# Two products of a linear-attention layer, put on 32-wide tiles of the TensorE array

## The chip, the cores and the metric

The kernel runs on one core of a Trainium2 chip. The metric is the device time of one execution in microseconds; medians of several runs are quoted. TensorE is the engine for matrix products; its results go to PSUM, a small memory that VectorE or ScalarE, the engines for element-wise work, must empty. A difference under 2% counts as "same".

## The reference

Four layers are applied in turn to an input of 2048 rows by 1024 columns: linear attention (A), a gated product (B), A again, B again. Only A matters here:

```python
phi = lambda t: jnp.where(t > 0, t + 1, jnp.exp(t)) + 1e-6
pq, pk = phi(q), phi(k)                          # 32 heads of 32 columns
kv  = jnp.einsum("bhsd,bhse->bhde", pk, v)       # one 32 x 32 block per head
z   = jnp.einsum("bhsd->bhd", pk)
num = jnp.einsum("bhqd,bhde->bhqe", pq, kv)
den = jnp.einsum("bhqd,bhd->bhq", pq, z)[..., None] + 1e-6
return (num / den, heads side by side) @ wo      # (shortened)
```

The kernel never forms `num`. Per layer it forms G = x^T·pk (the "g units"), from it k^T v = wv^T·G per head (the "kv units"), then M = (k^T v)·wo, a 1024 x 1024 matrix, and the output is (pq/den)·M. Each head needs only a 32 x 32 block of k^T v.

## The kernel before

The parts that the change touches. The array is 128 x 128, a chunk `c` holds four heads, and the products of one head with another are computed too and then masked away.

```python
def both(ps, lhsT, rhs, start, stop):            # two matmuls of 512 columns
    for n in range(2):
        nc.tensor.matmul(out=ps[:, n, :], lhsT=lhsT, rhs=rhs[:, n * NB:(n + 1) * NB], start=start, stop=stop)

def kv_unit(m):                                  # m = 0..7, accumulates over m
    def run():
        # ... psum tile "kv" [128, 8, 128] at m == 0
        for c in range(KD):
            nc.tensor.matmul(out=acc[0][:, c, :], lhsT=wkv[:, m, c * P:(c + 1) * P],
                             rhs=Gs[m % 2][:, c * P:(c + 1) * P], ...)
        if m == KD - 1:
            for h in range(2):                   # keep the four 32x32 diagonal blocks of each chunk
                nc.vector.tensor_tensor(out=KVb[:, 4 * h:4 * h + 4, :], in0=acc[0][:, 4 * h:4 * h + 4, :],
                                        in1=mask[:].unsqueeze(1).to_broadcast([P, 4, P]), op=ALU.mult)

def q_with_m(t, later):                          # last q unit, M woven in
    # ... PSUM tiles
    for c in range(KD):
        if c == 2: step(c)                       # step: two matmuls of the q unit
        pm = pss[(0, 1, 0, 2, 1, 0, 2, 0)[c]]
        both(pm, KVb[:, c, :], wo[c], True, True)     # M: 16 matmuls of 128x512 in all
        # ... copy pm to M on ScalarE or VectorE
        if c != 2: step(c)
    # ...

# ... order of the units on TensorE:
do([g[0], g[1], z_sum, kv[0]] + d(0) + [g[2], kv[1]] + d(1, 2) + [g[3], kv[2]] + ...)
# ...
do(d(8) + [q[2], g[6], kv[5]] + ... + [g[7], kv[6], q[5], kv[7], q[6]])
q_with_m(15, later)
```

`d(t)` is the division by `den`: about 4.2 us of VectorE work per block of 128 rows. `Gs` has two buffers.

## Time and profile before

| | before |
|---|---|
| device time, median | 1630.16 us (4 runs, 1629.41 to 1630.41) |
| profiled span | 1627.6 us |
| TensorE busy | 1622.9 us, 7649 matmuls |
| a 512-column matmul, start to start | 0.216 us |
| a kv unit, first start to the next unit's first start | 0.447 us |
| "stretch": first z matmul to first output-projection matmul, one layer | 76.52 us |

From the page of the kernel before, its busy times, then the chain of waits by engine:

```profile
span 1627.6 us, 17734 instructions
PE 1622.9 (100%) x7649; PEld 741.2 (46%) x7649; DVE 609.3 (37%) x889; ACT 289.3 (18%) x387; POOL 55.2 (3%) x141
...
PE 99%; DMA 0%; DVE 0%; issue 0%; SPq 0%
```

A busy TensorE may still be waiting inside, because a matmul's recorded duration (379 ns for 512 columns) overlaps the next one's. Start times decide. The timeline of TensorE alone has start, duration of the merged piece, engine, source line, operation, operands, shapes and count:

```profile
133.77 7.07 PE L202 MATMUL ps<-R,R 128*128 128x512 bf16 x32
140.68 0.61 PE L303 MATMUL kv<-GL,W 128*128 128x128 bf16 x8
141.12 3.62 PE L202 MATMUL ps<-W,xT 128*128 128x512 bf16 x16
```

The 32 matmuls of a g unit take 140.68 - 133.77 = 6.91 us, 0.216 us each. The eight of the kv unit take 0.45 us and the next unit starts at once. There is no bubble. The same view where M is made:

```profile
173.54 0.59 PE L202 MATMUL pm<-W,KVb 128*128 128x512 bf16 x2
173.98 0.59 PE L202 MATMUL ps<-W,xT 128*128 128x512 bf16 x2
174.41 0.59 PE L202 MATMUL ps<-W,KVb 128*128 128x512 bf16 x2
...
180.02 0.59 PE L202 MATMUL ps<-W,xT 128*128 128x512 bf16 x2
180.45 1.24 PE L202 MATMUL ps<-R,xT 128*128 128x512 bf16 x5
```

M (operand `KVb`) and the last q unit alternate, every pair 0.43 us after the one before. From 173.54 to 180.45 are 6.91 us for 32 matmuls, half of them M's: 16 x 0.216 = 3.46 us.

### The profile page before, as it was taken

The numbers are of one execution on the slowest core, as the hardware profiler recorded it, in microseconds if no ns is written. First come the engines' busy times: TensorE is split into PE (matmuls) and PEld (weight loads), VectorE is DVE, ScalarE is ACT, GpSimd is POOL, SyncE is SP. The second block draws the span as 40 slices with busy tenths as digits, with TensorE's granted clock in tenths as the row PEclk, the third lists the DMA queues.
The fourth block names the chain that finished last, engine by engine and source line by source line (L and its number), as shares of the span: only waits on it lengthen the run. The fifth ranks groups of instructions, "written<-read, shape, count | busy, mean of one in ns | idle before, by whom it ended". The sixth has DMA issues, their size and how long they took to land.

```text
span 1627.6 us, 17734 instructions
## 1 busy us (share of the span) xinstructions
PE 1622.9 (100%) x7649; PEld 741.2 (46%) x7649; DVE 609.3 (37%) x889; ACT 289.3 (18%) x387; POOL 55.2 (3%) x141
## 2 busy tenths in 40 slices
PE   9999999999999999999999999999999999999999
PEld 4444444444444444444444444444444444444444
DVE  6889853212311321243245798432123113211111
ACT  5533201101110110011045222011011101101110
POOL 2100000000000000010000000000000000000000
PEclk9999999999999999999999999999999999999999
DMA  7324856511550452142420248565236406511400
GB/s 238 54 72 104 233 162 172 165 52 52 163 173 1 137 161 91 52 154 65 93 52 1 78 104 233 156 174 161 69 92 175 136 20 172 165 65 65 155 0 27
DMA packets 235742, 182.82 MB, mean 112 GB/s; under 512 B 101264, under 2 KB 216464, under 8 KB 235664
## 3 DMA queue, kind: packets, MB, share of 16 engines
q1 hardware_dynamic: 235664, 181.69, 39.0%
q8 instruction: 60, 0.98, 0.3%
q14 instruction: 18, 0.15, 0.0%
HBM read 153.09 MB, written 4.19 MB: 97 GB/s over the span
## 4 chain that ended last, share of the span: by engine, by line
PE 99%; DMA 0%; DVE 0%; issue 0%; SPq 0%
PE ps L202 50%; PE ps L489 48%; PE ps L516 1%; PE kv L303 0%; PE pm L202 0%; DMA X<-in_A_x_dram 0%; PE pt L372 0%; DVE xT L375 0%; DVE st L181 0%; DVE R L359 0%; SPq L107 0%; DVE X L497 0%; DVE mv L183 0%
## 5 line engine op out<-in xcount | busy, mean ns | idle before, releaser
L489 PE MATMUL ps<-xT,R 128*128 128x512 bf16 x2432 | 528.5, 379 | 0.0
L489 PEld LDWEIGHTS <-R 128*128 128x128 bf16 x2432 | 238.0, 98 | 286.9
L493 DVE TENSOR_TENSOR R<-gs,ps 128x512 bf16<-128x512 f32 x224 | 154.0, 687 | 533.4 <-ACT gs L492 533.4
L202 PEld LDWEIGHTS <-R 128*128 128x128 bf16 x2248 | 219.8, 98 | 264.3
L492 ACT COPY gs<-ps 128x512 f32<-128x512 f32 x224 | 131.3, 586 | 1039.2 <-PE ps L489 1039.2
L489 PE MATMUL ps<-xT,W 128*128 128x512 bf16 x1152 | 251.6, 379 | 0.0
L202 PEld LDWEIGHTS <-xT 128*128 128x128 bf16 x1536 | 149.6, 98 | 178.3 <-DVE xT L375 0.7
L202 PE MATMUL ps<-W,xT 128*128 128x512 bf16 x1024 | 225.9, 379 | 0.3 <-DVE xT L375 0.3
L489 PEld LDWEIGHTS <-W 128*128 128x128 bf16 x1152 | 112.7, 98 | 135.9
L202 PE MATMUL ps<-W,R 128*128 128x512 bf16 x744 | 170.7, 379 | 0.0
L497 DVE TENSOR_TENSOR X<-X,ps 128x1024 bf16<-128x1024 bf16 (+3 forms) x34 | 39.4, 1159 | 335.7 <-PE ps L202 326.0
L202 PE MATMUL ps<-R,R 128*128 128x512 bf16 x512 | 112.8, 379 | 0.0
L202 PE MATMUL ps<-PQ,R 128*128 128x512 bf16 x496 | 112.1, 379 | 0.0
L202 PE MATMUL ps<-R,xT 128*128 128x512 bf16 x512 | 110.8, 379 | 0.0
L207 ACT ACTIVATE e<-ps 128x1024 bf16<-128x1024 f32 x56 | 57.4, 1024 | 145.4 <-PE ps L202 145.4
L181 DVE BATCH_NORM_STATS2 st<-X 128x6 f32<-128x512 bf16 x128 | 82.0, 682 | 2.1 <-DMA X<-in_A_x_dram 1.9
L185 POOL TENSOR_SCALAR ve<-mv 128x1 f32<-128x1 f32 x64 | 16.7, 260 | 1332.3 <-DVE mv L183 1332.3
L202 PE MATMUL ps<-xT,R 128*128 128x512 bf16 x248 | 58.6, 379 | 0.0
L202 PE MATMUL ps<-GL,R 128*128 128x512 bf16 x248 | 58.6, 379 | 0.0
L343 DVE TENSOR_TENSOR X<-X,ps 128x1024 bf16<-128x1024 bf16 x32 | 38.8, 1213 | 28.0 <-PE ps L202 28.0
L192 DVE TENSOR_SCALAR R<-X,mv,rstd 128x1024 bf16<-128x1024 bf16 x64 | 33.9, 542 | 24.0 <-POOL rstd L187 24.0
L211 DVE TENSOR_SCALAR e<-e 128x1024 bf16<-128x1024 bf16 x64 | 27.0, 422 | 39.0 <-ACT e L207 39.0
(64 smaller groups left out, 459.9 us busy)
## 6 DMA issues: line engine op xcount, KB each, us to landing
R<-in_B_w_gate_dram SPq DMA_DIRECT2D x38, 1024.0 KB, 5.5
R<-in_B_w_up_dram SPq DMA_DIRECT2D x38, 1024.0 KB, 7.5
W<-in_B_w_gate_dram SPq DMA_DIRECT2D x18, 1024.0 KB, 5.4
W<-in_B_w_up_dram SPq DMA_DIRECT2D x18, 1024.0 KB, 7.3
W<-in_A_wqkv_dram SPq DMA_DIRECT2D x10, 1024.0 KB, 6.3
W<-in_B_w_down_dram SPq DMA_DIRECT2D x6, 1024.0 KB, 11.3
PQ<-in_B_w_down_dram SPq DMA_DIRECT2D x4, 1024.0 KB, 8.1
X<-in_A_x_dram SPq DMA_DIRECT2D x15, 256.0 KB, 5.4
```

What stands on the lines that cost most here:

```text
L181: nc.vector.bn_stats(out=st[:, c, :], in_=X[:, t, c * NB:(c + 1) * NB])
L185: nc.gpsimd.tensor_scalar(out=ve[:], in0=mv[:, 1:2], scalar1=1e-5, scalar2=None, op0=ALU.add)
L192: nc.vector.tensor_scalar(out=dst, in0=X[:, t, :], scalar1=mv[:, 0:1], scalar2=rstd[:], op0=ALU.subtract, op1=ALU.mult)
L202: nc.tensor.matmul(out=ps[:, n, :], lhsT=lhsT, rhs=rhs[:, n * NB:(n + 1) * NB], start=start, stop=stop)
L207: nc.scalar.activation(out=e[:], in_=flat(ps), func=ACT.Exp, **sc)
L211: nc.vector.tensor_scalar(out=e[:], in0=e[:], scalar1=1.0, scalar2=EPS, op0=ALU.min, op1=ALU.add)
L343: nc.vector.tensor_tensor(out=X[:, t, :], in0=X[:, t, :], in1=flat(ps), op=ALU.add)
L489: nc.tensor.matmul(out=ps[:, n, :], lhsT=w[:, k, j * P:(j + 1) * P], rhs=xT[g % 2][:, k, :], start=(k == 0), stop=(k == KD - 1))
L492: nc.scalar.copy(out=gs[:], in_=ps[:, 0, :])
L493: nc.vector.tensor_tensor(out=hT[:, f, :], in0=gs[:], in1=ps[:, 1, :], op=ALU.mult)
L497: nc.vector.tensor_tensor(out=X[:, t, a:b], in0=X[:, t, a:b], in1=ps, op=ALU.add)
L516: nc.tensor.matmul(out=ps[:, 0, 0:b - a], lhsT=hT[:, f, tl * P:(tl + 1) * P], rhs=wd[f][:, a:b], start=(f == 0), stop=(f == KF - 1))
```

## The change

The intent is to stop computing what is masked away. M is computed by 16 array tiles of 32 x 32 at a time, each with the block of one head: one "quarter" of M is 16 small matmuls over 512 columns, and there are four quarters. So that the blocks lie on the right partitions, k^T v is computed by four tiles of 128 x 32 side by side, one head per matmul: 32 small matmuls per kv unit instead of 8. The mask goes. `wo` is loaded in another order of rows, and the last units are put in another order.

```diff
-    KVb = const.tile([P, KD, P], BF16, tag="KVb", name="KVb")
+    KVb = const.tile([P, 2, 4, DH], BF16, tag="KVb", name="KVb")
 # ... wo in eight DMAs of 32 partitions, not two of 128
         def g_unit(m):
 # ... every g unit now makes one half of its columns after the other (before: both halves for each t);
 # ... the last (m == 7) is copied out in two halves, each as soon as it is done
         def kv_unit(m):
-                for c in range(KD):
-                    nc.tensor.matmul(out=acc[0][:, c, :], lhsT=wkv[:, m, c * P:(c + 1) * P],
-                                     rhs=Gs[m % 2][:, c * P:(c + 1) * P], ...)
+                for h in range(2):
+                    for j in range(4):
+                        for r in range(4):
+                            a = (4 * h + r) * P + j * DH
+                            nc.tensor.matmul(out=acc[0][DH * r:DH * r + DH, h, j, :], lhsT=wkv[:, m, a:a + DH],
+                                             rhs=Gs[m % 2][:, a:a + DH], ..., tile_position=(0, DH * r))
                 if m == KD - 1:
-                    for h in range(2):
-                        nc.vector.tensor_tensor(... mask ...)
+                    nc.vector.tensor_copy(out=KVb[:], in_=acc[0][:])
-        def q_with_m(t, later):
+        def last_q_with_m(later):
+            qs = [mm_tile(), mm_tile()]
+            wide = mm_tile()
+            bank = [psum.tile([P, NB], F32, tag=f"kv{i}", bufs=1, name="pm") for i in range(2)]
+            def quarter(h, n, two):
+                for j in range(4):
+                    for r in range(4):
+                        o = bank[r][DH * j:DH * j + DH, :] if r < 2 else two[DH * j:DH * j + DH, r - 2, :]
+                        nc.tensor.matmul(out=o, lhsT=KVb[DH * r:DH * r + DH, h, j, :],
+                                         rhs=wo[h][DH * r:DH * r + DH, j, n * NB:(n + 1) * NB],
+                                         start=True, stop=True, tile_position=(DH * r, DH * j))
+            # ... returns take(copy, r), which copies a bank (or both banks of `two`) to M
+            take = quarter(0, 0, qs[1])
+            # ... takes on VectorE and ScalarE
+            steps(0, 0, 4)                       # 8 matmuls of a q unit
+            take = quarter(0, 1, wide)
+            # ... steps(0, 4, 8), quarter(1, 0, wide), steps(1, 0, 4), quarter(1, 1, wide), steps(1, 4, 8)
-        do(... + [g[7], kv[6], q[5], kv[7], q[6]])
-        q_with_m(15, later)
+        do(... + [g[7], kv[6], kv[7], q[5]])
+        last_q_with_m(later)
```

More of the change, by code (lines that the diff above doesn't have):

```diff
@@ L83 @@
     wq = rows(W2[:], D)
-    wo = [W3[:, c * D:(c + 1) * D] for c in range(4)] + [PQ[1][:, c * D:(c + 1) * D] for c in range(4)]
+    wo = [rows(W3[:], D), rows(PQ[1][:], D)]
     pq = [PQ[0][:, i * D:(i + 1) * D] for i in range(4)] + [PQ[1][:, i * D:(i + 1) * D] for i in range(4)]
@@ L98 @@
     wqkv_v = A_wqkv.rearrange("(k p) n -> p k n", p=P)
-    wo_v = A_wo.rearrange("(k p) n -> p k n", p=P)
+    wo_v = A_wo.rearrange("(s r j e) n -> s r e j n", s=2, r=4, j=4)
     wg_v = B_w_gate.rearrange("(k p) n -> p k n", p=P)
@@ L123, in load_o @@
     def load_o(h):
-        load(rows((W3 if h == 0 else PQ[1])[:], D), wo_v[:, 4 * h:4 * h + 4, :])
+        for r in range(4):
+            load(wo[h][DH * r:DH * r + DH, :, :], wo_v[h, r])
     def load_gu(i):
@@ L153 @@
     nc.gpsimd.memset(ones[:], 1.0)
-    mask = const.tile([P, P], F32, tag="mask", name="mask")
-    nc.gpsimd.memset(mask[:], 0.0)
-    for b in range(P // DH):
-        nc.gpsimd.memset(mask[DH * b:DH * b + DH, DH * b:DH * b + DH], 1.0)
     warm = const.tile([P, 1], F32, tag="warm", name="warm")
@@ L289, in run @@
             def run():
-                ps = mm_tile()
-                for t in range(NT):
-                    both(ps, XN[:, t, m * P:(m + 1) * P], PK[:, t, :], t == 0, t == NT - 1)
-                nc.scalar.copy(out=Gs[m % 2], in_=flat(ps))
+                for n in range(2):
+                    if n == 0 or m == KD - 1:
+                        ps = mm_tile()
+                    for t in range(NT):
+                        nc.tensor.matmul(out=ps[:, n, :], lhsT=XN[:, t, m * P:(m + 1) * P],
+                                         rhs=PK[:, t, n * NB:(n + 1) * NB], start=(t == 0), stop=(t == NT - 1))
+                    if m == KD - 1:
+                        nc.scalar.copy(out=Gs[m % 2][:, n * NB:(n + 1) * NB], in_=ps[:, n, :])
+                if m < KD - 1:
+                    nc.scalar.copy(out=Gs[m % 2], in_=flat(ps))
             return run
@@ L300, in run @@
                 if m == 0:
-                    acc[:] = [psum.tile([P, KD, P], F32, tag="kv", bufs=1, name="kv")]
-                for c in range(KD):
-                    nc.tensor.matmul(out=acc[0][:, c, :], lhsT=wkv[:, m, c * P:(c + 1) * P],
-                                     rhs=Gs[m % 2][:, c * P:(c + 1) * P],
-                                     start=(m == 0 and c % 4 == 0), stop=(m == KD - 1), skip_group_check=True)
+                    acc[:] = [psum.tile([P, 2, 4, DH], F32, tag="kv0", bufs=1, name="kv")]
@@ new lines, in run @@
+                for h in range(2):
[3 more added lines that the diff above has]
+                            nc.tensor.matmul(out=acc[0][DH * r:DH * r + DH, h, j, :], lhsT=wkv[:, m, a:a + DH],
+                                             rhs=Gs[m % 2][:, a:a + DH], start=(m == 0 and h == 0 and j == 0),
+                                             stop=(m == KD - 1), tile_position=(0, DH * r), skip_group_check=True)
@@ L306, in run @@
                 if m == KD - 1:
-                    for h in range(2):
-                        nc.vector.tensor_tensor(out=KVb[:, 4 * h:4 * h + 4, :], in0=acc[0][:, 4 * h:4 * h + 4, :],
-                                                in1=mask[:].unsqueeze(1).to_broadcast([P, 4, P]), op=ALU.mult)
-            return run
-        def q_with_m(t, later):
-            pss = [psum.tile([P, 2, NB], F32, tag="kv", bufs=1, name="pm"), mm_tile()]
-            ps = mm_tile()
-            pss.append(mm_tile())
-            tl = t % TPG
-            def step(c):
-                both(ps, xT[t // TPG][:, c, tl * P:(tl + 1) * P], wq[:, c, :], c == 0, c == KD - 1)
-            for c in range(KD):
-                if c == 2:
-                    step(c)
-                pm = pss[(0, 1, 0, 2, 1, 0, 2, 0)[c]]
-                both(pm, KVb[:, c, :], wo[c], True, True)
-                if c % 2:
-                    nc.scalar.copy(out=M[:, c, :], in_=flat(pm))
-                else:
-                    nc.vector.tensor_copy(out=M[:, c, :], in_=flat(pm))
-                if c != 2:
-                    step(c)
-                if c in (2, 4):
-                    later.pop(0)()
-            phi(ps, q_slot(t), scale_of(t))
@@ new lines, in run, with steps, take @@
+                    nc.vector.tensor_copy(out=KVb[:], in_=acc[0][:])
+            return run
+        def last_q_with_m(later):
+            qs = [mm_tile(), mm_tile()]
+            wide = mm_tile()
+            bank = [psum.tile([P, NB], F32, tag=f"kv{i}", bufs=1, name="pm") for i in range(2)]
+            def steps(i, a, b):
+                t = 14 + i
+                tl = t % TPG
+                for c in range(a, b):
+                    both(qs[i], xT[t // TPG][:, c, tl * P:(tl + 1) * P], wq[:, c, :], c == 0, c == KD - 1)
+            def quarter(h, n, two):
+                for j in range(4):
+                    for r in range(4):
+                        o = bank[r][DH * j:DH * j + DH, :] if r < 2 else two[DH * j:DH * j + DH, r - 2, :]
+                        nc.tensor.matmul(out=o, lhsT=KVb[DH * r:DH * r + DH, h, j, :],
+                                         rhs=wo[h][DH * r:DH * r + DH, j, n * NB:(n + 1) * NB],
+                                         start=True, stop=True, tile_position=(DH * r, DH * j))
+                def take(copy, r):
+                    cols = slice(n * NB, (n + 1) * NB)
+                    if r < 2:
+                        copy(out=M[:, 4 * h + r, cols], in_=bank[r][:])
+                    else:
+                        copy(out=M[:, 4 * h + 2:4 * h + 4, cols], in_=two[:])
+                return take
+            dve, act = nc.vector.tensor_copy, nc.scalar.copy
+            take = quarter(0, 0, qs[1])
+            take(dve, 0)
+            take(dve, 1)
+            take(act, 2)
+            steps(0, 0, 4)
+            take = quarter(0, 1, wide)
+            take(dve, 0)
+            take(dve, 1)
+            take(act, 2)
+            steps(0, 4, 8)
+            take = quarter(1, 0, wide)
+            take(act, 0)
+            take(act, 1)
+            take(dve, 2)
+            phi(qs[0], q_slot(14), scale_of(14), later)
+            steps(1, 0, 4)
+            take = quarter(1, 1, wide)
+            take(dve, 0)
+            take(dve, 1)
+            take(dve, 2)
+            do(later)
+            steps(1, 4, 8)
+            phi(qs[1], q_slot(15), scale_of(15))
@@ L367, in turn_pe @@
                         continue
-                    tag, bufs = ("mm", 3) if h else ("kv", 1)
+                    tag, bufs = ("mm", 3) if h else ("kv0", 1)
                     pt = psum.tile([P, KD, P], BF16, tag=tag, bufs=bufs, name="pt")
@@ L450, in layer_A @@
         later = []
-        q[5], q[6] = q_unit(13, later), q_unit(14, later)
+        q[5] = q_unit(13, later)
         do([g[0], g[1], z_sum, kv[0]] + d(0) + [g[2], kv[1]] + d(1, 2) + [g[3], kv[2]] + d(3) + [q[0]] + d(4))
@@ L455, in layer_A @@
         load_o(1)
-        do(d(8) + [q[2], g[6], kv[5]] + d(9, 10) + [q[3]] + d(11) + [q[4]] + d(12) + [g[7], kv[6], q[5], kv[7], q[6]])
-        q_with_m(15, later)
+        do(d(8) + [q[2], g[6], kv[5]] + d(9, 10) + [q[3]] + d(11) + [q[4]] + d(12) + [g[7], kv[6], kv[7], q[5]])
+        last_q_with_m(later)
         load_gu(0)
```

## The prediction

> **What bounds the kernel.** TensorE. The page gives PE 1622.9 of 1627.6 us busy and the chain of waits 99% PE. Busy alone proves little, so I read start times in the timeline: 512-column matmuls start every 0.216 us (32 in 6.91 us) and no stage touched by the change has a bubble. VectorE (37%) and ScalarE (18%) keep up. Time changes only by what TensorE's stream gains or loses.
>
> **What the change touches, per linear-attention layer (there are two).**
> 1. M = (k^T v)·wo: 16 matmuls of 128x512 with a block-diagonal operand, 16 x 0.216 = 3.46 us. They become four quarters of 16 tile matmuls of 32x32 over 512 columns. The Trainium skill ("TensorE: Matmul & The Clock Gate", Part 3) says that such tiles run concurrently and gives 10.6x for 16. With free weight loads a quarter would take little over one 0.216 us stream; with 16 loads and issues I estimate 0.45 us, 1.8 us in all: gain about 1.6 us. No trace here shows tiles yet.
> 2. k^T v: eight units of 8 matmuls, 128x128 over 128 columns, 0.45 us each in the timeline, 3.6 us a layer. They become 32 matmuls of 128x32 over 32 columns: four times the loads and matmuls, each too short to hide its fixed cost. The skill ("TensorEngine Tiling", Instruction Overhead and Restrictions) puts a floor of about 60 cycles under a matmul and says column tiling loses the fast weight load. Four tiles overlapping would give about 0.4 us, fully serial ones 1 us or more. Estimate 0.6 us: loss 1.2 us.
> 3. Tiling-mode switches drain the array (same page, Key Properties): seven k^T v stretches and four quarters, two switches each, 22 a layer. Estimate 0.05 us each, partly hidden, from a matmul's 379 ns duration against 216 ns spacing: loss 1.1 us.
> 4. Masking goes: two 0.69 us VectorE operations become one copy (estimate 0.4 us). A 3.45 us q unit hides either.
> 5. New possible stalls: the last k^T v unit follows g[7] with only kv[6] to hide ScalarE's copy (1.01 us when whole, hence the split); the shared PSUM tile `wide` waits for q[5]'s Exp and Relu (2 x 1.02 us) against about 2.1 us of TensorE work. Estimate 0.3 us. M's evictions move the same columns in 12 instead of 8 copies; VectorE has slack (9.3 of 14.5 us busy there).
> 6. wo in eight smaller DMAs instead of two: over 20 us early, off the path.
>
> **Sum.** Per layer -1.6 +1.2 +1.1 +0.3 = +1.0; twice, +2 us. The schedule looks hand-fitted, which makes me lean to the better end of items 2 and 3 (tiles overlap, switches cheap): -1 us. Nothing reaches 2% (32 us): item 1 can save at most 6.9 us.
>
> Predicted 1629 us; 8 in 10 between 1623 and 1640. Faster by over 2%: 0.01; within 2%: 0.97; slower by over 2%: 0.02.
>
> **What would show it.** Timeline: a quarter of M takes 0.3 to 0.6 us of PE start time; a k^T v unit 0.4 to 0.9 us; steps around them still 0.216 us a matmul; gap at a switch under 0.1 us. PE instructions rise by 2 x (48 + 192) = 480. Other stages unchanged.
>
> **What would make it wrong.** Weight loads of column tiles that cannot overlap a running matmul of the same row group: then a k^T v unit takes 1.5 us and a quarter as long as before (0.86 us), +17 us. Or a 0.2 us switch: +7 us. The other way: tiles that overlap perfectly, -6 us. Or waits for `wide` or the two `pm` banks, if evictions run behind VectorE's division work.

## The result, and the profile after

Ratios in this document are the mean time of one kernel's fast runs over the mean time of the other's fast runs of the same rounds, so not quite the ratio of the medians quoted.

| | before | after |
|---|---|---|
| device time, median | 1630.16 us | 1626.60 us (4 runs, 1626.45 to 1627.47) |
| ratio | | 0.998, 95% interval 0.9965 to 0.9995 |
| profiled span | 1627.6 us | 1624.7 us |
| stretch, one layer (both layers alike) | 76.52 us | 74.91 us |

The stretches of two layers give 2 x 1.61 = 3.2 us. The profiled spans differ by only 2.9 us, because the profiled run of the change lost about half a microsecond in its first 8 us, where TensorE's work is the same in both (the k matmuls after the second block of start-up transposes begin at 7.74 us, against 7.21 us before). I count that to the single execution and not to the change: in `m_row_order`, whose start-up is that of the change, they begin at 7.08 us. The medians differ by 3.6 us.

From the page after:

```profile
span 1624.7 us, 18711 instructions
PE 1620.1 (100%) x8129; PEld 735.3 (45%) x8129; DVE 609.4 (38%) x895; ACT 287.3 (18%) x389; POOL 54.5 (3%) x136
...
PE 100%; ACT 0%; DVE 0%; issue 0%
```

TensorE executes 8129 - 7649 = 480 more matmuls and is done sooner. The timeline of a kv unit alone, and of the last two with what follows:

```profile
134.16 7.07 PE L291 MATMUL ps<-R,R 128*128 128x512 bf16 x32
141.16 0.38 PE L310 MATMUL kv<-GL,W 128*32 128x32 bf16 x32
141.47 0.82 PE L199 MATMUL ps<-W,xT 128*128 128x512 bf16 x3
...
166.16 0.53 PE L310 MATMUL kv<-GL,W 128*32 128x32 bf16 x48
166.90 0.28 PE L310 MATMUL kv<-GL,W 128*32 128x32 bf16 x16 [0.21 <-ACT GL L294]
167.11 3.63 PE L199 MATMUL ps<-W,xT 128*128 128x512 bf16 x16
170.67 0.39 PE L334 MATMUL pm<-W,KVb 32*32 32x512 bf16 x2
170.67 0.39 PE L334 MATMUL ps<-W,KVb 32*32 32x512 bf16 x2
...
171.03 1.90 PE L199 MATMUL ps<-W,xT 128*128 128x512 bf16 x8
...
177.63 1.90 PE L199 MATMUL ps<-W,xT 128*128 128x512 bf16 x8
179.37 0.81 PE L199 MATMUL ps<-R,xT 128*128 128x512 bf16 x3
```

Read three things. The kv unit takes 141.47 - 141.16 = 0.31 us, but the g unit ahead of it took 7.00 us from start to start, not 6.91. A quarter of M takes 171.03 - 170.67 = 0.37 us. In the last kv unit TensorE stands still for ScalarE's copy of the last g unit (`GL`); the note says 0.21 us because it counts from a modelled end, while start times show a gap of 0.396 us. That is the only new wait of TensorE (the same view of the kernel before has none on `GL`); the view of its waits has it in both layers:

```profile
PE ps L169 <- DVE xT L164: 1.2, 1, 1.2
PE kv L310 <- ACT GL L294: 0.4, 2, 0.2
PE ps L199 <- DVE xT L409: 0.3, 1, 0.3
```

The merged timeline hides single starts. These are the gaps from each matmul's start to the next, read from the records of the same trace, in ns:

```
g unit            ... 216 216 | 309 (last one, to the first of the kv unit)
kv unit, 32       4 3 3 30 | 3 3 4 15 | 3 3 4 15 | ... (six rounds of 25) ... | 3 3 4
leaving it        108 (to the next unit's first) 226 216 216 ...
q step            ... 216 | 309
quarter, 16       3 3 4 3 3 4 3 3 4 3 3 4 3 3 4
leaving it        317 226 216 ...
kv[6] then kv[7]  309 | 32 starts within 0.20 us | 19, then 7 to 12 each | 396 (the wait) | 16 starts | 108
```

Going into tiles costs 309 - 216 = 93 ns. Coming out costs about as much: 108 ns where the round would have gone on after 15, or 317 where a stream of 512 columns takes 216, and 10 ns more at the next matmul. So a layer's gain is, against 76.52 us:

- a kv unit standing alone: 93 + 308 + 10 - 447 = -36 ns, six of them: -0.22 us;
- the last two, with one switch pair and the wait: 93 + 951 + 10 - 894 = +160 ns;
- a quarter: 93 + 367 + 11 - 864 = -393 ns, four of them: -1.57 us.

The sum is -1.63 us, and the stretch says -1.61. The first theory from this ledger is that **the 16 tiles of M bring nearly all of the gain, and k^T v on tiles brings almost nothing, because the switches into and out of tile mode and one wait take back what the tiles save**. A rival is that k^T v brings about half, or that the gain comes from the new order of the units.

### The profile page after: what moved, and what is told of

The parts are those of the page before. It is cut to its first block, busy times and chain, and to the rows that moved or that the text cites. A ratio compares the mean times of both kernels' runs of the same rounds, so it can differ in the third digit from the quotient of the medians.

```text
span 1624.7 us, 18711 instructions
## 1 busy us (share of the span) xinstructions
PE 1620.1 (100%) x8129; PEld 735.3 (45%) x8129; DVE 609.4 (38%) x895; ACT 287.3 (18%) x389; POOL 54.5 (3%) x136
## 4 chain that ended last, share of the span: by engine, by line
PE 100%; ACT 0%; DVE 0%; issue 0%
PE ps L523 48%; PE ps L199 44%; PE ps L291 7%; PE ps L550 1%; PE kv L310 0%; PE ps L169 0%; PE pm L334 0%; PE pt L406 0%; ACT GL L294 0%; DVE xT L409 0%; DVE X L531 0%; DVE xT L164 0%; PE ps L334 0%
```

## The experiments

Twelve kernels ran on the chip, in four groups, each with its own runs of the kernel before (medians 1629.53 to 1629.92 us). All were correct. Stretches are of one layer, from the profile; both layers agreed within 0.01 us, those of `kv_tiles_dve` within 0.03. Later traces lack a few per cent of the matmul records; a missing one shows as a gap of 431 ns and was not taken for a wait.

| label | median us | ratio to before | stretch us |
|---|---|---|---|
| before | 1629.5 to 1629.9 | 1 | 76.52 |
| changed_again | 1626.29 | 0.9980 | 74.91 |
| m_tiles_only | 1630.63 | 1.0006 | 77.00 |
| m_tiles_act | 1627.16 | 0.9985 | 75.26 |
| kv_tiles_only | 1633.15 | 1.0021 | 78.18 |
| kv_tiles_two | 1632.54 | 1.0016 | 77.82 |
| kv_tiles_dve | 1629.76 | 1.0000 | 76.53 |
| kv_same_tile | 1626.80 | 0.9986 | 75.17 |
| kv_split | 1628.80 | 0.9995 | 76.18 |
| m_row_order | 1625.89 (1 run) | none | 74.91 |
| kv_after_q | 1625.52 | 0.9975 | 74.54 |
| kv_pairs | 1628.13 | 0.9991 | 75.75 |
| kv_pairs_early_div | 1624.72 | 0.9969 | 74.17 |

### The change once more

No edit.

> The changed kernel itself, as the reference of this round. Ratio to the kernel before 0.998 as on the first chip, stretch from the start of the last z matmuls to the first output-projection matmul 74.9 us in both layers (76.5 before).

It repeated: 1626.29 us against 1629.75, ratio 0.998 (0.9968 to 0.9993), stretch 74.91 us.

### M on tiles alone

The changed kernel with k^T v put back to 128 x 128; the head blocks, which then lie on other partitions, are copied out one by one.

```diff
-   # 32 matmuls of 128x32 per kv unit
+   for c in range(KD):
+       nc.tensor.matmul(out=acc[0][:, c // 4, c % 4, :], lhsT=wkv[:, m, c * P:(c + 1) * P],
+                        rhs=Gs[m % 2][:, c * P:(c + 1) * P], ...)
-   nc.vector.tensor_copy(out=KVb[:], in_=acc[0][:])
+   for i in range(16):
+       j, r = i // 4, i % 4
+       copy = nc.vector.tensor_copy if i % 3 == 2 else nc.scalar.copy
+       copy(out=KVb[DH * r:DH * r + DH, :, j, :], in_=acc[0][DH * j:DH * j + DH, :, r, DH * j:DH * j + DH])
```

> The changed kernel with k^T v put back to 8 matmuls of 128x128 per unit (its head blocks then copied out one by one); M stays on 16 array tiles. Theory 1 (M's tiles carry nearly all the gain; k^T v by tiles is neutral because two mode switches eat it): each linear-attention stretch, from the start of the last z matmul to the first output-projection matmul, is shorter than in the kernel before by 4 x 0.393 = 1.57 us, less a wait of about 0.17 us for the last copy of g[7]: 1.40 us a layer, 2.8 us in all, so about 1627.4 us. Rival (the k^T v tiles carry about half of the gain): only 0.8 us a layer, 1.6 us in all. The spacing of the 128-column k^T v matmuls must be 56 ns and no 309 ns gap may stand before them.

It missed: 1630.63 us, and a stretch of 77.00 us. The trace shows a fault of the experiment. From TensorE's waits and its timeline, `m_tiles_only`:

```profile
PE pm L336 <- ACT KVb L314: 3.6, 2, 1.8
```

```profile
172.75 0.39 PE L336 MATMUL pm<-W,KVb 32*32 32x512 bf16 x2 [1.81 <-ACT KVb L314]
```

Each copy on one engine waited for the one on the other, so 16 copies of 0.2 us took 5 us and M's first quarter came 1.81 us late. The longest single wait had another cause: VectorE was still in a division when its first copy fell due, and ScalarE's third copy stood 1.71 us until it was made. After that the two took turns, with waits of 0.48 and 0.28 us. From the timeline of all engines:

```profile
168.16 1.22 DVE L281 TENSOR_TENSOR PQ<-PQ,den 128x1024 bf16<-128x1024 bf16 x1
169.41 0.22 DVE L314 CAST KVb<-kv 32x64 bf16<-32x64 f32 x1
169.66 0.41 ACT L314 CAST KVb<-kv 32x64 bf16<-32x64 f32 x2 [1.71 <-DVE KVb L314]
```

This run decides nothing. It was repeated with one engine:

```diff
-       copy = nc.vector.tensor_copy if i % 3 == 2 else nc.scalar.copy
-       copy(out=KVb[...], in_=acc[0][...])
+       nc.scalar.copy(out=KVb[...], in_=acc[0][...])
```

> m_tiles_only again without its own fault: there the 16 block copies went to VectorE and ScalarE in turn, each waited for the other, and TensorE stood 1.81 us a layer. Now all 16 are on ScalarE (16 x 0.21 us from the end of k^T v, while q[5] runs for 3.45 us). Theory 1 as before: stretch 76.52 - 1.40 = 75.1 us, 2.8 us less than the kernel before in all. Rival (half of the gain is from k^T v): 75.7 us.

1627.16 us; stretch 75.26 us, where 75.1 was expected and the rival said 75.7. Two gaps of its own remain: 0.168 us before the second half of the last kv unit (a start gap of 224 ns instead of 56; it was in the expectation, as 0.17) and 0.134 us before the first quarter (443 ns instead of 309), because the 16 copies took 3.43 us and not 16 x 0.21 = 3.36, and end just too late. Without both the stretch would be 74.96, which is 1.57 us under the kernel before; four quarters at 0.393 us make 1.57. M's tiles by themselves account for the gain.

### k^T v on tiles alone

The kernel before with only its kv units changed, the blocks then copied into the block-diagonal operand.

```diff
-   # 8 matmuls of 128x128 per kv unit, then two multiplications by the mask
+   # 32 matmuls of 128x32 as in the change, then 16 block copies into a zeroed KVb
+       copy = nc.vector.tensor_copy if i % 3 == 2 else nc.scalar.copy
+       copy(out=KVb[DH * j:DH * j + DH, :, r, DH * j:DH * j + DH], in_=acc[0][DH * r:DH * r + DH, :, j, :])
```

> The kernel before with only its k^T v units put on four column tiles of 128x32 (blocks then copied into the block-diagonal operand), its M untouched. Theory 1: each unit costs 0.309 + 0.309 + 0.010 instead of 0.216 + 0.447 us, 36 ns less, so the stretch is 0.29 us shorter per layer, 0.6 us in all, about 1629.6 us. Rival of theory 1 (half the gain from here): 1.6 us less in all. The terms of the recorded prediction (loss of 1.2 us in the units and 0.7 us in their switches a layer) would make it 3.8 us longer.

1633.15 us, stretch 78.18 us. This looks like the terms of the recorded prediction (78.4) and is not: TensorE waited 1.8 us a layer for the same kind of copies (the first began only at 171.35 us, when ScalarE was done with Exp and Relu of a q unit; then they took turns), and its kv units ran as fast as in the change. A second form gave each engine its own destination tile:

```diff
-   KVb = const.tile([P, 2, 4, P], ...)
+   KVb = [const.tile([P, 2, 2, P], ...) for i in range(2)]
+   # r < 2: VectorE into KVb[0]; r >= 2: ScalarE into KVb[1]
```

> kv_tiles_only again without its own fault (there, block copies on two engines waited for each other and kept TensorE 1.8 us a layer): the block-diagonal operand is two tiles, one filled by VectorE and one by ScalarE. Theory 1 (k^T v by tiles, its switches counted, is worth 36 ns a unit): stretch 76.52 - 0.29 = 76.23 us, 0.6 us in all. Rival (about half of the change's gain comes from here): 75.7 us. The recorded prediction's terms (loss of 1.9 us a layer): 78.4 us.

1632.54 us, stretch 77.82 us: another miss. TensorE still waited 1.4 us a layer: ScalarE's first copy again stood behind Exp and Relu, and then the engines still took turns. From `kv_tiles_two`, the timeline of VectorE, then of ScalarE:

```profile
172.51 0.45 DVE L311 CAST KVb<-kv 32x64 bf16<-32x64 f32 x2 [1.58 <-ACT KVb L311]
173.44 0.45 DVE L311 CAST KVb<-kv 32x64 bf16<-32x64 f32 x2 [0.49 <-ACT KVb L311]
```

```profile
172.99 0.42 ACT L311 CAST KVb<-kv 32x64 bf16<-32x64 f32 x2 [0.51 <-DVE KVb L311]
173.93 0.42 ACT L311 CAST KVb<-kv 32x64 bf16<-32x64 f32 x2 [0.52 <-DVE KVb L311]
```

The destinations are now apart; what the copies still share is the PSUM tile that they read. That this sharing is what the waits are for was argued from here and not tested. The third form uses one engine, and moves one step of the last q unit ahead of M:

```diff
+   nc.vector.tensor_copy(out=KVb[r // 2][...], in_=acc[0][...])      # all 16
-   if c == 2: step(c)
+   if c in (0, 2): step(c)
```

> The kernel before with only its k^T v units on column tiles, third form: all 16 block copies on VectorE, which is idle then (16 x 0.225 = 3.6 us after the last unit), and one step of the last q unit moved ahead of M's first matmul to cover them. In the two forms before, the copies on two engines waited for each other. Theory 1 (a k^T v unit by tiles is worth 36 ns, its two switches counted): stretch 76.52 - 0.29 = 76.23 us. Rival (half of the gain): 75.7 us. The recorded prediction's terms: 78.4 us.

1629.76 us, ratio 1.000 (0.9986 to 1.0014); stretch 76.53 us. Two gaps of its own are in it. In the first layer they are 122 ns before M's first matmul and 183 ns before its third pair (start gaps of 338 and 399 instead of 216). The first is the end of VectorE's copies (170.30 + 3.74 = 174.04 us). The second comes from the moved step: M's first and third pair use one PSUM tile (`pm`), they now stand one step closer, and the third starts when VectorE has just emptied the tile:

```profile
174.77 1.23 DVE L332 CAST R<-pm 128x1024 bf16<-128x1024 f32 x1 [0.73 <-PE pm L200]
...
176.04 0.59 PE L200 MATMUL pm<-W,KVb 128*128 128x512 bf16 x2
```

Taken out they leave 76.54 - 0.305 = 76.24 us (in the second layer 76.51 - 0.27, the same), 0.01 us from the figure of theory 1. So k^T v on tiles is worth 0.29 us a layer if nothing waits for it, and nothing at all as it was built here. The rival (half of the gain) falls: it asked for 75.7.

The other rival, the new order of the units, was not run alone. The trace of the kernel before answers it: in both layers' stretches, the start after any 512-column matmul follows at 215 or 216 ns. No order of the same matmuls had a gap to close there; what the new order brought is the wait in the last kv unit.

### The cost of a switch

The same instructions as in the change, but the second half of six kv units a layer is issued in the middle of a later g unit: six more stretches of tile matmuls.

```diff
         def g_unit(m):
                 for n in range(2):
+                    if n == 1 and 2 <= m:
+                        kv_half(m - 2, 1)
 # ...
-                for h in range(2):               # kv_unit: both halves at once
+                kv_half(m, *((0,) if m < KD - 2 else (0, 1)))
```

> The changed kernel with the second half of six of the eight k^T v units of a layer moved into the middle of a later g unit: the same instructions, but 6 more stretches of tile matmuls a layer. Theory (a round trip into and out of tile mode costs 309 - 216 = 93 ns going in and 108 - 15 + 10 = 103 ns coming out): +0.196 x 12 = +2.35 us over the changed kernel. Rival (these gaps belong to the unit, as first loads or last drains that any matmul of its size has): half units cost half, +0.3 us at most.

1628.80 us, some 2.2 to 2.5 us over the changed kernel of the other groups (2.35 expected). The stretch rose by 76.18 - 74.91 = 1.27 us for six extra round trips: 0.21 us each, where 0.196 was expected. The rival (gaps that belong to a unit's work) is out. From the timeline of `kv_split`:

```profile
108.67 0.28 PE L308 MATMUL kv<-GL,W 128*32 128x32 bf16 x16
108.87 3.63 PE L293 MATMUL ps<-R,R 128*128 128x512 bf16 x16
112.43 0.28 PE L308 MATMUL kv<-GL,W 128*32 128x32 bf16 x16
```

The 16 matmuls between the two halves take 112.43 - 108.87 = 3.56 us, where 16 x 0.216 = 3.46; and half a kv unit takes 0.208 us by its single starts, two thirds of a whole one (0.308 us).

### Four small matmuls in a row on one tile

```diff
-                    for j in range(4):
-                        for r in range(4):
+                    for r in range(4):
+                        for j in range(4):
```

> The changed kernel with the two inner loops of a k^T v unit swapped, so that four matmuls in a row go to the same column tile instead of to four different ones. Same instructions, same result. Theory (a tile needs about 25 ns per small matmul, and the four tiles do that side by side): a unit's 32 starts take 32 x 25 = 0.8 us instead of 0.2, +0.6 us for each of 16 units, +9.6 us over the changed kernel, about 1636 us. Rival (the rate is set by issue, or loads and matmuls are pulled ahead whatever the tile): unchanged within 0.5 us.

The theory failed: 1626.80 us, not 1636 (four runs, one of them 1629.16). From the timeline of `kv_same_tile`:

```profile
141.02 0.41 PE L310 MATMUL kv<-GL,W 128*32 128x32 bf16 x32
141.37 0.82 PE L199 MATMUL ps<-W,xT 128*128 128x512 bf16 x2
```

A unit takes 0.35 us instead of 0.31. The records don't name the tile, but by the program's order the first four starts are on one tile, and they lie 14, 13 and 12 ns apart; after that two runs of such steps overlap, as if a second tile worked between them: 238 ns for 31 gaps. So 25 ns is not what a small matmul costs a tile. A reading that fits both orders is that a tile needs 12 to 13 ns to stream 32 columns and as much to take new weights, and hides the latter when another matmul of the same tile stands next in line; no run tests that reading.

### Four tiles of one row group in a row

The prediction named one thing that would ruin the gain: weights that cannot load while another tile of the same row group streams.

```diff
-                for j in range(4):
-                    for r in range(4):
+                for r in range(4):
+                    for j in range(4):
                         o = bank[r]... if r < 2 else two...
```

> The changed kernel with M's two tile loops swapped: four tiles of one row group in a row, instead of one tile of each row group in turn. Theory (a tile's weights load while another tile of the same row group streams, as k^T v's column tiles do): the 16 starts of a quarter stay 3 to 4 ns apart and a quarter stays 0.367 us from first start to the next q matmul. Rival (loads overlap a running matmul only in another row group): [...]a quarter takes 0.86 us or more, +2 us a layer.

The 16 starts stayed 3 to 4 ns apart, and the stretch stayed at 74.91 us. From the timeline of `m_row_order`:

```profile
169.69 0.38 PE L199 MATMUL ps<-W,xT 128*128 128x512 bf16 x1
170.00 0.41 PE L334 MATMUL pm<-W,KVb 32*32 32x512 bf16 x8
170.03 0.41 PE L334 MATMUL ps<-W,KVb 32*32 32x512 bf16 x8
170.37 0.82 PE L199 MATMUL ps<-W,xT 128*128 128x512 bf16 x3
```

170.37 - 170.00 = 0.37 us a quarter, as before. The worry was groundless.

### Taking the wait away

The changed kernel, with the last two kv units behind q[5] and M's quarters each one half of a q unit later (with the PSUM tiles, and the engines that empty them, dealt out anew).

```diff
-  [g[7], kv[6], kv[7], q[5]]
+  [g[7], q[5], kv[6], kv[7]]
   # last_q_with_m:
-  quarter(0, 0, qs[1]), steps(0, 0, 4), quarter(0, 1, wide), steps(0, 4, 8), quarter(1, 0, wide),
-  steps(1, 0, 4), quarter(1, 1, wide), steps(1, 4, 8)
+  steps(0, 0, 4), quarter(0, 0, qs[1]), steps(0, 4, 8), quarter(0, 1, wide),
+  steps(1, 0, 4), quarter(1, 0, wide), steps(1, 4, 8), quarter(1, 1, qs[0])
```

> The changed kernel with the last two k^T v units moved behind q[5] (so that ScalarE's copy of g[7] is hidden by q[5], no longer awaited), and M's quarters each one half q unit later. Theory (TensorE's 0.38 us gap inside the last k^T v unit is the wait for that copy, and nothing else is waiting behind it): stretch 74.91 - 0.38 = 74.53 us, 0.76 us off the changed kernel's time. Rival (the wait moves on: the copy of k^T v or an eviction of M now ends last): unchanged, with a gap of some 0.3 us before a quarter.

Stretch 74.54 us, 0.01 off; 1625.52 us, 0.8 us under the changed kernel of the same rounds. The 0.38 us were that wait and nothing came in its place.

### Fewer switches

`kv_after_q` with the kv units in pairs: four stretches of kv matmuls a layer in place of seven.

```diff
-  [g[0], g[1], z_sum, kv[0]] + d(0) + [g[2], kv[1]] + d(1, 2) + [g[3], kv[2]] + d(3) + [q[0]] + d(4)
-  [g[4], kv[3]] + d(5, 6) + [q[1], g[5], kv[4]] + d(7)
+  [g[0], g[1], z_sum, kv[0], kv[1]] + d(0) + [g[2]] + d(1, 2) + [g[3]] + d(3) + [q[0], kv[2], kv[3]] + d(4)
+  [g[4]] + d(5, 6) + [g[5], q[1], kv[4], kv[5]] + d(7)
   # g[6], kv[5] becomes g[6]; the g unit copied in halves is g[1]
```

> kv_after_q with the k^T v units in four pairs, 4 stretches of tile matmuls a layer in place of 7. Theory (0.196 us a round trip, as the split test put it at 0.21): another 3 x 0.196 = 0.59 us a layer; stretch 73.95 us, 1.9 us off the changed kernel in all, about 1624.7 us. If the switches cost less than thought, or the copy of g[1] is awaited in the first pair, the gain over kv_after_q is under half of this.

Worse than the change: 1628.13 us. From `kv_pairs`, TensorE's first quarter and, 30 us earlier, the cause on VectorE:

```profile
172.66 0.39 PE L334 MATMUL pm<-W,KVb 32*32 32x512 bf16 x2 [1.51 <-DVE KVb L314]
```

```profile
136.67 1.23 DVE L281 TENSOR_TENSOR PQ<-PQ,den 128x1024 bf16<-128x1024 bf16 x1
141.49 0.43 DVE L208 TENSOR_SCALAR e<-e 128x1024 bf16<-128x1024 bf16 x1 [3.60 <-ACT e L204]
```

VectorE took its work in the program's order. With q[1] later on TensorE, VectorE stood 3.60 us at the first operation of q[1] while a division was ready behind it. It never caught up, and its copy of k^T v came late. The cure is to put the division ahead:

```diff
-  ... + d(3) + [q[0], kv[2], kv[3]] + d(4)
+  ... + d(3, 4) + [q[0], kv[2], kv[3]]
-  [g[4]] + d(5, 6) + [g[5], q[1], kv[4], kv[5]] + d(7)
+  [g[4]] + d(5, 6, 7) + [g[5], q[1], kv[4], kv[5]]
```

> kv_pairs with two division units moved ahead of the q units in VectorE's order. In kv_pairs VectorE stood 3.6 us waiting for q[1], fell behind by as much, and its copy of k^T v kept TensorE 1.51 us before M's first quarter. Theory: that wait goes, and what remains of the pairs is 3 merges at 0.14 us, not 0.196, because after 33 load-and-matmul pairs in a row the spacing rises from 6.4 to 8.3 ns a matmul (start times of kv_pairs). Stretch 74.54 - 0.41 = 74.13 us, so 0.8 us less than kv_after_q in all, ratio to before about 0.997. Rival (pairs bring waits of their own that the 1.51 us hid): stretch 74.5 us or more.

Stretch 74.17 us where 74.13 was expected; 1624.72 us (1624.66 to 1625.17), ratio to before 0.9969 (0.9956 to 0.9981). The division now fills the hole and the copy of k^T v is early. From the timeline of `kv_pairs_early_div`, VectorE, and then VectorE and TensorE at the end:

```profile
140.15 1.23 DVE L281 TENSOR_TENSOR PQ<-PQ,den 128x1024 bf16<-128x1024 bf16 x1
141.64 0.43 DVE L208 TENSOR_SCALAR e<-e 128x1024 bf16<-128x1024 bf16 x1 [0.27 <-ACT e L204]
```

```profile
169.55 0.42 DVE L314 CAST KVb<-kv 128x256 bf16<-128x256 f32 x1 [1.39 <-PE kv L310]
...
171.23 0.39 PE L334 MATMUL pm<-W,KVb 32*32 32x512 bf16 x2
```

This version beats both kernels, by 5.2 us the one before and by about 1.6 to 1.9 us the change: still "same" by the 2% rule, and the two ratios' intervals overlap (0.9968 to 0.9993 for the change). It is the stretches, 74.17 against 74.91 us in both layers, that tell them apart.

One merge saved (74.54 - 74.17) / 3 = 0.12 us and not the 0.196 that a round trip costs. Start times show why: the first 33 matmuls of a stretch come at 25 ns for four; all later ones come 8.4 ns apart, so the second unit of a pair takes about 0.27 us and not 0.20.

## Why the prediction was right or wrong

The time (1626.6 us) lies in the range 1623 to 1640, and nothing reached 2%. That proves little: 1630.16 us, no change at all, lies in the range too. And the point was 2.4 us too high: a change of about -1 us was forecast and -3.6 us measured. The sum over a layer shows that it came as near as it did by luck, because its errors offset each other:

| term, per layer | predicted | measured | from |
|---|---|---|---|
| M on tiles, without switches | -1.6 us | -2.39 us | 4 x (0.367 - 0.101 - 0.864) |
| k^T v on tiles, without switches | +1.2 us | -1.79 us | six alone at 0.215, the last two 0.495 together (in `kv_after_q`), against 8 x 0.447 |
| switches | +1.1 us | +2.19 us | 7 x 0.196 and 4 x 0.205 |
| new waits | +0.3 us | +0.36 us | the last kv pair, 0.951 instead of 0.595 us |
| sum | +1.0 us | -1.63 us | stretch: -1.61 us |

1. **TensorE bounds the kernel, and only its stream counts.** Right. The stretch changes by what its start times change by, and the smaller VectorE work (one copy of 0.42 us for two multiplications of 0.69 us) shows nowhere.
2. **M's tiles.** The mechanism was right, the size low: a quarter was put at 0.45 us. It takes 0.367 us from its first start to the next q matmul, and 0.101 us of that is the way out of tile mode. The Trainium skill ("TensorE: Matmul & The Clock Gate", Part 3) says that tiles start about 4 ns apart; here it was 3 to 4 ns, so 16 starts take 0.05 us, and loading weights did not stretch them. The 10.6x that the prediction quotes for 16 tiles was not measured as such; a quarter's 16 streams one after another would take 16 x 0.216 = 3.46 us (an estimate), 13 times the 0.266 us of a quarter without its switches and 7 times the 0.47 us with them.
3. **k^T v on tiles: the step that failed.** The prediction said "Estimate 0.6 us: loss 1.2 us". It put a floor of about 60 cycles under every small matmul, as the Trainium skill has it ("TensorEngine Tiling", Instruction Overhead), and took the loads as partly serial. The runs showed 32 loads and matmuls in 0.2 us, and the unit with its way out in 0.31 us, against 0.447 before and the 0.4 to 0.9 us that the prediction asked the timeline to show. The sign of the term was wrong.
4. **Switches.** That mode switches drain the array is what the skill says ("TensorEngine Tiling", Key Properties), without a figure. The trace fits that and gives one: 93 ns in and about 103 ns out. Draining itself is not seen in it. What the records do show is that a weight load loses its head start at a switch: among the 128 x 128 matmuls it starts some 214 ns ahead of its own matmul, but 1 ns ahead going in (141.161 and 141.162 us) and 4 ns coming out (141.466 and 141.470). Whether the drain or the late load sets the 93 ns, no run tells. The prediction had 0.05 us for each, half of it. `kv_split` shows that the cost goes with the number of switches. It eats nearly the whole gain of k^T v on tiles: 0.23 us a unit saved, 0.196 us paid.
5. **New waits.** The size was nearly right, the place half right. The wait for ScalarE's copy of g[7] exists, and `kv_after_q` removed all of it. The wait for `wide` never came: all four quarters start 309 ns after the last q matmul.
6. **`wo` in eight DMAs.** Right that it stays off the path: no quarter waits for a load.

The sum was +2 us for both layers; the prediction then leaned to -1 us, its reason being "The schedule looks hand-fitted". The lean went the right way, but it rested on no measurement, and no run supports it as a reason.

What stays open: why a load-and-matmul pair on its own tile needs 25 ns in rotation and 12 to 14 ns in a row; and whether the slower rate after 33 pairs comes from the queue of waiting instructions. The skill gives TensorE a queue of 64 entries ("TensorE: Matmul & The Clock Gate", the table at its head), which 33 pairs would just exhaust; that is an argument, and no run was made to vary it. The change's own trace speaks for it without proving it: in the last two kv units the spacing rises to about 8.6 ns after 32 starts, and after the wait of 396 ns, in which instructions could queue up again, the last 16 come at 25 ns for four once more.

## What to carry to other kernels

Small array tiles side by side are cheap in themselves; what they cost is the way into the mode and out of it, about 0.2 us for a round trip here, so gather tile matmuls into few stretches, and expect a short product that is already dense in columns to break even. When TensorE has no bubble, write the ledger in start-to-start times of single matmuls: it foretold five of these stretches to 0.05 us or better (`m_row_order`, `kv_after_q` and `kv_pairs_early_div`, and `m_tiles_act` and `kv_tiles_dve` once their own gaps were counted). It was 0.09 us off in `kv_split`, and wrong on `kv_same_tile`. And an experiment that undoes half of a change needs its own glue, whose waits must be taken out before its time says anything.

## What the Trainium skill lacked or had wrong

- "TensorE: Matmul & The Clock Gate", Part 1, has a floor of about 25 ns from start to start, however few columns, and "TensorEngine Tiling", Instruction Overhead, an overhead of about 60 cycles for each matmul; neither makes an exception for tiles where it stands, though Part 3 has about 4 ns between starts on different tiles. Here matmuls of 32 columns followed each other on one column tile every 12 to 14 ns (`kv_same_tile`, by the program's order), and on different tiles every 3 to 4 ns, as Part 3 says.
- "TensorE: Matmul & The Clock Gate", Part 3, The mechanism: weight loads overlap running matmuls only where the row group differs (though the same section also lets a load go ahead into a background weight buffer). Here they overlapped within one row group: in a kv unit, whose column tiles use all rows, the records have a weight load starting 2 ns after the first matmul, and the four tiles' matmuls start 3 to 4 ns apart; `m_row_order` put four tiles of one row group in a row and lost nothing.
- "TensorEngine Tiling", Key Properties: a switch of tiling mode drains the array, with no figure. Here it was 93 ns going in and 103 to 112 ns coming out, 0.2 us a round trip (0.21 us in `kv_split`).
- No page has a rate for a long run of tile matmuls. Here, after 33 load-and-matmul pairs in a row, the spacing rose from 25 ns for four to 8.4 ns for each.
